# Thirty-two unused bytes in front of each weight slice of a fused attention and MLP kernel

## The chip, the cores and the metric

The kernel runs on one core of one Trainium2 chip. The metric is the device time of one execution in microseconds (us). A core has a matrix engine (PE, whose loads of the stationary operand are listed apart as PEld), three elementwise engines (DVE, ACT, POOL), a sequencer that issues most transfers (SP), and 16 DMA engines. Operands of the engines lie in the on-chip memory: 128 partitions, in each of which a buffer has the same byte address. Matmuls write to PSUM, a second small memory. This case is about the byte addresses of some of those buffers alone.

## The reference

Chunked attention on 4 batches, 8 heads, 768 positions and 64 values a head, and behind it an MLP on the 3072 tokens with 512 inputs, 2048 hidden units and 512 outputs, all in 32-bit floats:

```
for c in range(nc):                       # 24 chunks of 32 queries
    k_ctx = k[:, :, l_start:r_end]        # 16 keys to the left, 8 to the right
    k_full = np.concatenate([mem_k, k_ctx], axis=2)    # and 8 memory keys
    scores = scale * np.matmul(q_c, k_full.transpose(0, 1, 3, 2))
    a = np.exp(scores - np.max(scores, axis=-1, keepdims=True))
    a = a / (np.sum(a, axis=-1, keepdims=True) + 1e-09)
    out[:, :, c_start:c_end] = np.matmul(a, v_full)
...
h = x @ w_in
g = np.maximum(h, 0.0) + alpha * np.minimum(h, 0.0)
return g @ w_out
```

## The kernel before

The tokens go through the MLP in seven blocks: four of 384 tokens, then three of 512. The hidden dimension is cut into 16 slices of 128 units (f = 0 to 15). A step of the program is one block with one slice: an up product (x times the slice of w_in, line 746), the bend of the leaky ReLU (lines 755 and 758), and a down product (the result times the slice of w_out, line 776), which adds to the block's output over all 16 slices.

To keep 32-bit accuracy on a faster matmul format, each operand is split in a high and a low part (xh and xl, gh and gl, and w with its index 0 or 1), and each product is three matmuls: high by low, low by high, high by high. In the up product the weight is the stationary operand, loaded 128 columns (512 bytes a partition) at a time, and x is streamed past it, 384 or 512 columns. In the down product it is the other way round: 128 columns of g are stationary and the 512 columns of w (2048 bytes a partition) are streamed.

The weights stay on the chip. Slice f has a buffer in a pool of its own, `w{f}_0` (8192 bytes a partition; slices 0 and 1 have two pools of 4096 bytes each, `w0_0`, `w0_1` and so on). Such a buffer has up to three tenants one after the other. Those of slices 8 to 15 first hold the queries, keys and values of the first eight attention units (tile `early`: lines 502 to 508 load it, lines 324 and 579 multiply it). Then the raw 64-bit weights land in each (tile `w_t`, line 620), and a decode of five to six instructions on ACT, DVE and POOL turns them into a high and a low part in the same place (lines 643 to 672, tile `w`; the last instruction, line 672, writes the low part). From there on every step reads them.

The order of the work is set by a planner (class `Plan`): each step has an engine, an assumed cost, the buffers that it reads and writes, and a due time, and the planner hands out the steps by a simulated schedule before the program is emitted. Addresses are no input to it.

Pools are laid out in the order in which they are opened, one behind the other. Before the change the x buffers (pool `xp`), the bent hidden values and their parts (pools `gp`, `dec`, `tmp`, and the spare thirds of `xp`) and all weight slices start at addresses that leave 416 when divided by 512. The pieces that matmuls of lines 746 and 776 read within them begin at multiples of 512 bytes, so stationary and streamed operand of each of these matmuls begin at the same address modulo 512.

Of the kernel before, what the change touches and what calls it, by code (L numbers as in the profile page):

```python
# [9 lines left out]
F32 = mybir.dt.float32  # L10
# [8 lines left out]
P = 128  # L19
# [14 lines left out]
NF = DF // P  # L34
# [81 lines left out]

NAPART = 2


GATHER_ACT, HIGH_ACT = range(2, 14), 24  # L120

# [63 lines left out]
def body(ctx: ExitStack, tc: tile.TileContext, qvw, kw, whole, heads, w_in, w_out, alpha, out):  # L185
# [7 lines left out]
    sm = ctx.enter_context(tc.tile_pool(name="sm", bufs=1))  # L193
    xp = ctx.enter_context(tc.tile_pool(name="xp", bufs=1))
    gp = ctx.enter_context(tc.tile_pool(name="gp", bufs=1))
    wps = {(f, i): ctx.enter_context(tc.tile_pool(name=f"w{f}_{i}", bufs=1))
           for f in range(NF) for i in range(2 if f < NAPART else 1)}
    dec = ctx.enter_context(tc.tile_pool(name="dec", bufs=1))
    tmp = ctx.enter_context(tc.tile_pool(name="tmp", bufs=1))
    ps_h = ctx.enter_context(tc.tile_pool(name="ps_h", bufs=1, space=bass.MemoryType.PSUM))  # L200
# [785 lines left out]
```

## Time and profile before

| | |
|---|---|
| time, median of 2 runs | 595.97 us (595.90 to 596.05) |
| span of the profiled execution, first to last instruction | 593.9 us |
| TensorE clock granted over the span | 1.000 |
| PE busy | 586.2 us (99%) |
| PEld busy | 503.4 us (85%) |
| DVE busy | 390.2 us (66%) |
| ACT busy | 207.8 us (35%) |
| POOL busy | 47.5 us (8%) |
| moved by DMA | 47.65 MB |

The profile is of one execution; its span is 2.1 us under the median of the times, which also hold what lies before the first and behind the last instruction. Times within a view count from the start of the span. A row of a group gives the line, engine, operation, the output tile, an arrow, the input tiles, sizes and count, then busy time and the mean duration in ns. Matmuls overlap, so the duration of one (389 ns for 512 columns) is longer than the distance from one to the next; that distance is read from the chain of waits, which lists runs of matmuls with their start, length and count.

### The profile page before, as it was taken

The numbers are of one execution on the slowest core, as the hardware profiler recorded it, in microseconds if no ns is written. First come the engines' busy times: TensorE is split into PE (matmuls) and PEld (weight loads), VectorE is DVE, ScalarE is ACT, GpSimd is POOL, SyncE is SP. The second block draws the span as 40 slices with busy tenths as digits, with TensorE's granted clock in tenths as the row PEclk, the third lists the DMA queues.
The fourth block names the chain that finished last, engine by engine and source line by source line (L and its number), as shares of the span: only waits on it lengthen the run. The fifth ranks groups of instructions, "written<-read, shape, count | busy, mean of one in ns | idle before, by whom it ended". The sixth has DMA issues, their size and how long they took to land.

```text
span 593.9 us, 10980 instructions
## 1 busy us (share of the span) xinstructions
PE 586.2 (99%) x4407; PEld 503.4 (85%) x4407; DVE 390.2 (66%) x905; ACT 207.8 (35%) x578; POOL 47.5 (8%) x74
## 2 busy tenths in 40 slices
PE   7999999999999999999999999999999999999997
PEld 4889898989998989989888888888888888888886
DVE  8979999886768768686895842851961771530530
ACT  3888887725131404424224202302400401210201
POOL 5640000010000101010010100100100100000000
PEclk9999999999999999999999999999999999999999
DMA  8999300222041221403304003004101000000001
GB/s 321 393 408 408 124 0 2 66 65 89 2 153 30 72 66 37 153 1 102 102 0 153 2 1 100 2 0 133 40 1 36 0 1 36 36 1 0 2 0 71
DMA packets 21187, 47.65 MB, mean 80 GB/s; under 512 B 2576, under 2 KB 5904, under 8 KB 21136
## 3 DMA queue, kind: packets, MB, share of 16 engines
q1 hardware_dynamic: 20992, 46.83, 22.2%
q8 instruction: 34, 0.56, 0.4%
q14 instruction: 17, 0.14, 0.1%
q10 hardware_dynamic: 144, 0.13, 0.1%
HBM read 40.66 MB, written 6.29 MB: 79 GB/s over the span
## 4 chain that ended last, share of the span: by engine, by line
PE 97%; DMA 1%; POOL 1%; issue 0%; ACT 0%; SPq 0%; ACTq 0%; POOLq 0%
PE h_ps L746 45%; PE o_ps L776 44%; PE a_ps L450 3%; PE s_ps L349 2%; PE a_ps L579 1%; DMA early<-heads 1%; PE o_ps L566 1%; POOL early L211 1%; PE s_ps L324 0%; POOL ew L232 0%; ACT o_t L833 0%; ACT qk L571 0%; POOL eye L225 0%; POOL eye L224 0%; SPq L505 0%
## 5 line engine op out<-in xcount | busy, mean ns | idle before, releaser
L746 PE MATMUL h_ps<-xh,w 128*128 128x384 f32 (+1 forms) x896 | 248.8, 358 | 0.0
L746 PEld LDWEIGHTS h_ps<-xh,w 128*128 128x128 f32 x896 | 164.9, 188 | 16.0
L776 PE MATMUL o_ps<-w,gh 128*128 128x512 f32 x528 | 162.8, 389 | 0.0
L746 PE MATMUL h_ps<-xl,w 128*128 128x384 f32 (+1 forms) x448 | 162.7, 363 | 0.0
L755 ACT ACTIVATE g<-h_ps 128x384 f32<-128x384 f32 (+1 forms) x112 | 60.3, 538 | 193.1 <-PE h_ps L746 127.3
L758 DVE SCALAR_TENSOR_TENSOR g<-g,rise,h_ps 128x384 f32<-128x384 f32 (+1 forms) x112 | 74.9, 669 | 74.3 <-ACT g L755 73.3
L776 PEld LDWEIGHTS o_ps<-w,gh 128*128 128x128 f32 x528 | 99.1, 188 | 20.5
L425 DVE STREAM_TRANSPOSE pt<-e 32x192 f32<-32x192 f32 (+1 forms) x336 | 99.4, 301 | 7.4 <-POOL e L404 2.0
L776 PE MATMUL o_ps<-w,gl 128*128 128x512 f32 x264 | 102.8, 389 | 0.0
L746 PEld LDWEIGHTS h_ps<-xl,w 128*128 128x128 f32 x448 | 84.1, 188 | 10.1
L776 PE MATMUL o_ps<-w,xh 128*128 128x512 f32 x240 | 74.8, 393 | 0.0
L776 PEld LDWEIGHTS o_ps<-w,gl 128*128 128x128 f32 x264 | 49.6, 188 | 10.2
L489 DVE TENSOR_TENSOR xl<-a_ps,xh 128x384 fp32r<-128x384 f32 x32 | 17.5, 553 | 59.0 <-ACT xh L486 58.4
L404 POOL TENSOR_TENSOR e<-e,den 128x384 f32<-128x384 f32 x24 | 22.4, 931 | 408.6 <-DVE den L401 272.4
L776 PEld LDWEIGHTS o_ps<-w,xh 128*128 128x128 f32 x240 | 45.0, 188 | 8.9
L764 DVE CAST gh<-g 128x512 fp32r<-128x512 f32 (+1 forms) x72 | 29.0, 403 | 30.6 <-PE o_ps L776 28.1
L383 ACT ACTIVATE e<-s_ps,mx 128x64 f32<-128x64 f32 x144 | 43.4, 319 | 14.2 <-DVE mx L375 14.2
L486 ACT CAST xh<-a_ps 128x384 fp32r<-128x384 f32 x32 | 15.0, 482 | 95.2 <-PE a_ps L450 93.2
L768 DVE TENSOR_TENSOR gl<-g,gh 128x512 fp32r<-128x512 f32 (+1 forms) x72 | 46.9, 653 | 1.8
L776 PE MATMUL o_ps<-w,xl 128*128 128x512 f32 x120 | 46.7, 389 | 0.0
L383 ACT ACTIVATION_READ_ACCUMULATOR e<-s_ps,mx 128x1 f32 x144 | 30.6, 213 | 0.0
L833 ACT COPY o_t<-o_ps 128x512 f32<-128x512 f32 x21 | 12.1, 589 | 40.2 <-PE o_ps L776 39.8
(61 smaller groups left out, 381.3 us busy)
## 6 DMA issues: line engine op xcount, KB each, us to landing
w_t<-w_in SPq DMA_DIRECT2D x16, 512.0 KB, 10.1
w_t<-w_out SPq DMA_DIRECT2D x16, 512.0 KB, 10.2
qk<-kw SPq DMA_DIRECT2D x24, 272.0 KB, 4.3
v_t<-qvw SPq DMA_DIRECT2D x24, 256.0 KB, 2.8
out<-o_t SPq DMA_DIRECT2D x23, 256.0 KB, 2.0
qk<-qvw SPq DMA_DIRECT2D x24, 192.0 KB, 4.7
early<-heads SPq DMA_DIRECT2D x14, 232.0 KB, 4.9
early<-qvw SPq DMA_DIRECT2D x8, 256.0 KB, 5.8
```

Source lines behind the costliest of these rows:

```text
L383: nc.scalar.activation(out=st["e"][:, i], in_=st["s"][h2][:, n], func=AF.Exp, scale=SCALE, bias=d["mx"][:, u - us[0], n, h2:h2 + 1], accum ...
L404: nc.gpsimd.tensor_tensor(out=st["e"], in0=st["e"], in1=st["den"].broadcast_to([P, NJ * 2, KW]), op=ALU.mult)
L425: nc.vector.transpose(out=pts[u % NPT][quad * CH:(quad + 1) * CH, j, t0:t0 + n1 - n0].rearrange("p t h q -> p (t h) q"), in_=(st["e"], zer ...
L450: nc.tensor.matmul(out=st["a"][h2 * D:(h2 + 1) * D, t * TQ:(t + 1) * TQ], lhsT=st["v"][:, t, h2, :], rhs=pts[u % NPT][:, :, t, h2, :], sta ...
L486: nc.scalar.copy(out=ring[k][0][:, cols], in_=st["a"][:, :BT])
L489: nc.vector.tensor_tensor(out=ring[k][1][:, cols], in0=st["a"][:, :BT], in1=ring[k][0][:, cols].bitcast(F32), op=ALU.subtract)
L746: nc.tensor.matmul(out=h["ps"][:, :n_cols], lhsT=ws[f, 0][:, wk, k * P:(k + 1) * P], rhs=parts(blk, k)[1](xk), start=(k == 0 and n == 0), ...
L755: nc.scalar.activation(out=h["g"], in_=h["ps"][:, :n_cols], func=AF.Relu, scale=-1.0)
L758: nc.vector.scalar_tensor_tensor(out=h["g"], in0=h["g"], scalar=rise[:, f:f + 1], in1=h["ps"][:, :n_cols], op0=ALU.mult, op1=ALU.add)
L764: copy(out=h["gh"], in_=h["g"])
L768: nc.vector.tensor_tensor(out=h["gl"], in0=h["g"], in1=h["gh"].bitcast(F32), op=ALU.subtract)
L776: nc.tensor.matmul(out=o_ps[tt], lhsT=h[gk][:, tt * P:(tt + 1) * P], rhs=ws[f, 1][:, wk], start=(f == first_f and i == 0), stop=(f == last ...
```

## The change

In front of each slice's buffer a small pool is opened, with one tile of 32 bytes a partition in it. Nothing ever writes or reads this tile.

```diff
+STEP = 32
...
-    wps = {(f, i): ctx.enter_context(tc.tile_pool(name=f"w{f}_{i}", bufs=1))
-           for f in range(NF) for i in range(2 if f < NAPART else 1)}
+    wps = {}
+    for f in range(NF):
+        shift = ctx.enter_context(tc.tile_pool(name=f"shift{f}", bufs=1))
+        shift.tile([P, STEP // 4], F32, name=f"shift{f}")
+        for i in range(2 if f < NAPART else 1):
+            wps[f, i] = ctx.enter_context(tc.tile_pool(name=f"w{f}_{i}", bufs=1))
```

Slice f moves up by 32 × (f + 1) bytes: modulo 512 the slices now start at 448, 480, 0, 32, 64 and so on, up to 384 and 416 for slices 14 and 15. The pools behind them (`dec`, `tmp`) move by 16 × 32 = 512 bytes and keep their 416; the pools in front do not move. The instructions of every engine, their order, their waits and their shapes are the same as before; nothing differs but the addresses inside them.

## The prediction

> **What bounds the kernel now.** I read the page first, for which engine sets the end, then the chain of waits for what the engine spends its time on, then the engine's own waits.
>
> ```profile
> span 593.9 us, 10980 instructions
> ...
> PE 586.2 (99%) x4407; PEld 503.4 (85%) x4407; DVE 390.2 (66%) x905; ACT 207.8 (35%) x578; POOL 47.5 (8%) x74
> ...
> PE 97%; DMA 1%; POOL 1%; issue 0%; ACT 0%; SPq 0%; ACTq 0%; POOLq 0%
> PE h_ps L746 45%; PE o_ps L776 44%; PE a_ps L450 3%; PE s_ps L349 2%; PE a_ps L579 1%; DMA early<-heads 1%; PE o_ps L566 1%; POOL early L211 1%; PE s_ps L324 0%; POOL ew L232 0%; ACT o_t L833 0%; ACT qk L571 0%; POOL eye L225 0%; POOL eye L224 0%; SPq L505 0%
> ```
>
> PE is 97% of the chain that ends last, and 89% of the span is the two weight products, lines 746 and 776. The waits of PE over the whole span are these three:
>
> ```profile
> PE h_ps L308 <- DVE busy L214: 2.0, 1, 2.0
> PE s_ps L324 <- DMA early<-heads: 1.2, 3, 0.6
> PE s_ps L324 <- DVE den L544: 0.7, 1, 0.7
> ```
>
> All three are in the opening with the attention units (lines 308 and 324). Afterwards nothing that another engine does is waited for, so the time can change much in one way only: the distance from one matmul to the next changes. The groups of PE by shape give the number of matmuls of which a weight slice is one operand:
>
> ```profile
> L776 PE MATMUL o_ps<-w,gh 128*128 128x512 f32 x528 | 162.8, 389 | 0.0
> L746 PE MATMUL h_ps<-xh,w 128*128 128x384 f32 x512 | 130.5, 335 | 0.0
> L746 PE MATMUL h_ps<-xh,w 128*128 128x512 f32 x384 | 118.3, 389 | 0.0
> L776 PE MATMUL o_ps<-w,gl 128*128 128x512 f32 x264 | 102.8, 389 | 0.0
> L746 PE MATMUL h_ps<-xl,w 128*128 128x384 f32 x256 | 87.5, 342 | 0.0
> L746 PE MATMUL h_ps<-xl,w 128*128 128x512 f32 x192 | 75.2, 392 | 0.0
> L776 PE MATMUL o_ps<-w,xh 128*128 128x512 f32 x240 | 74.8, 393 | 0.0
> L776 PE MATMUL o_ps<-w,xl 128*128 128x512 f32 x120 | 46.7, 389 | 0.0
> ```
>
> The counts add up to 2496 (768 of 384 columns, 1728 of 512). The chain in order of time gives their distances; its columns are start, length, what, count:
>
> ```profile
> 78.62 2.10 PE h_ps L746 x12
> 80.72 2.08 PE o_ps L776 x9
> ...
> 149.76 6.26 PE h_ps L746 x36
> ...
> 546.77 21.76 PE h_ps L746 x96
> 568.53 21.77 PE o_ps L776 x96
> ```
>
> At the end of the span 96 matmuls of 512 columns take 21.76 us, 226.7 ns each, whether the weight is stationary (line 746) or streamed (line 776). Thirty-six of 384 columns take 6.26 us, 173.9 ns each. The difference is 52.8 ns for 128 columns, 0.412 ns a column; 512 columns at this rate are 211 ns, which leaves some 15 ns a matmul that don't depend on its length (rounding of the rows makes that 14 to 16). Earlier, at 80.72, nine matmuls of 512 columns take 2.08 us, 231.1 ns each: 4.4 ns more than at the end. Two rows of busy time by stretch show what differs between the two places:
>
> ```profile
> 40.00:70.00 30.00, 30.00 (x153) 27.33 (x152) 28.01 (x39) 25.60 (x32) 1.28 (x2) 1.00 0.82 325
> ...
> 500.00:594.00 94.00, 90.29 (x404) 74.39 (x400) 30.98 (x50) 14.72 (x26) 0.00 (x0) 1.00 0.06 23
> ```
>
> Columns are the stretch, its length, busy time of PE, PEld, DVE, ACT and POOL, the granted clock and the DMA share. In the early stretch DVE is busy 28.01 of 30.00 us and DMA 0.82 of the time; in the late one 30.98 of 94.00 and 0.06; the clock is 1.00 in both. So a matmul is slowed a little, by 4.4 ns in 227, by something that other users of the memory do. That is the only sign in this trace that the memory is felt by PE at all.
>
> **The change part by part.** It removes no instruction and adds none, no wait and no transfer. It moves sixteen buffers, and with them the addresses in four kinds of instructions. I take each kind for itself.
>
> *Matmuls and weight loads of lines 746 and 776.* Before, the stationary and the streamed operand begin at the same address modulo 512; now they differ by 32 to 480 bytes in 15 slices, and slice 15 (416 again) stays as it was. So 15/16 of 2496, 2340 matmuls, are touched. Can the start distance matter? A row of the weight loads:
>
> ```profile
> L776 PEld LDWEIGHTS o_ps<-w,gh 128*128 128x128 f32 x528 | 99.1, 188 | 20.5
> ```
>
> A load goes through 512 bytes a partition and takes 188 ns, under a matmul that goes through 2048 bytes in 227 ns. While one load lasts, the stream advances by some 2048 × 188/227 = 1700 bytes and the load by 512: their distance grows by about 1190 bytes, more than twice 512. Whatever distance the two begin with, every distance modulo 512 comes up twice during each load (once or less, if part of the 188 ns is only delay). If meeting at some distance cost anything, it would be met before and after the change alike. I therefore take nothing for this term. Its bounds from rows: the 15 ns that don't depend on the length are all that a better address could give back, 2340 × 15 ns = 35.1 us; as much again is my bound above. These ends are the rivals below and not part of the likely case.
>
> [...]
>
> *Crowding by other engines.* The 4.4 ns are paid where slices are decoded and loaded. The down matmuls whose other operand is in xh or xl are for the most part the early ones: 240 + 120 = 360, × 4.4 ns = 1.6 us. The up matmuls of that time go at 2.10/12 = 175.0 ns against 173.9, 1.1 ns more; for some 400 of them that is 0.4 us. Together 2.0 us: other addresses could take it away or double it. I take no change, since the decode writes and reads whole 8192-byte buffers and so passes over all addresses modulo 512 in any case. If the cover is gone (a neighbour that now always meets PE), it is the 2.0 us again.
>
> [...]
>
> *The decode (lines 643 to 672).* Its instructions read and write the moved buffers on ACT, DVE and POOL. It has next to no slack at slice 2, the first whose low part DVE makes:
>
> ```profile
> 39.57 1.23 DVE L672 TENSOR_TENSOR w<-a,w 128x1024 fp32r<-128x1024 f32 x1 [0.65 <-ACT w L667]
> ...
> 40.83 0.34 PE L746 MATMUL h_ps<-xl,w 128*128 128x384 f32 x1
> 40.85 0.35 PEld L746 LDWEIGHTS h_ps<-xh,w 128*128 128x128 f32 x2
> ```
>
> DVE ends at 39.57 + 1.23 = 40.80, the first up matmul with this slice starts at 40.83 and the load of its low part at 40.85. A decode that is slower by some time up to here would thus hold PE for that time, once. How much one such instruction varies with its surroundings:
>
> ```profile
> L672 DVE TENSOR_TENSOR w<-a,w x14: 1182/1220/1227, 39.6 to 119.4; 128x1024 fp32r<-128x1024 f32 x14
> ...
> 20.00:40.00 20.00, 20.00 (x186) 17.47 (x179) 17.31 (x35) 16.77 (x34) 12.46 (x20) 1.00 1.03 406
> ```
>
> From 1182 to 1227 ns is 4%. Four per cent of DVE's 17.31 us between 20 and 40 us is 0.7 us, either way. All new addresses are still multiples of 32 bytes, as the old ones were, and the shapes are the same; I take nothing.
>
> *The loads into the buffers.* `early<-heads` is 1% of the chain, and PE waits 1.2 us on it. The two rows that say what the loads of weights cost later:
>
> ```profile
> early<-heads SPq DMA_DIRECT2D x14, 232.0 KB, 4.9
> ...
> w_t<-w_in SPq DMA_DIRECT2D x16, 512.0 KB, 10.1
> ```
>
> After the opening PE waits for no transfer, so the weights' 10.1 us to landing are covered by the decode that runs ahead and the work on slices that are there. For the opening I bound the term by its wait: 1.2 us less if it went, 1.2 us more if it doubled. The two halves of one such load already land at two different addresses modulo 512 (2176 bytes apart), and no slice's buffer was on a multiple of 512 before. I take nothing.
>
> The sum: 0 from the matmuls, 0 ± 2.0 from crowding, 0 ± 0.7 from the decode, 0 ± 1.2 from the opening, so 0 ± 3.9 us on the span of 593.9. What lies around the span (595.97 − 593.9 = 2.1 us) is untouched. The forecast is 596.0 us, from 592.1 to 599.9.
>
> **The rivals.** First, the common address is what costs the 15 ns, and the change gives them back. For it: the 15 ns are there in each matmul, in both roles of the weight, and before the change no matmul of lines 746 and 776 has operands at different addresses modulo 512, so the trace can't exclude it. Against it: the distance sweeps over all values during each load, as worked out above, and the same 15 ns for 384 and 512 columns look like a cost of changing the stationary operand. Its time: 596.0 − 35.1 = 561 us in full; it counts as faster by 2% (11.9 us) from 11.9/2340 = 5.1 ns a matmul.
>
> Second, the other side: the common address is the good one. Load and stream start within a few ns of each other; now they begin at the same place and part, and with a start distance of a few hundred bytes the stream, which is the quicker, overtakes the load in the middle instead of at its end. Place: each of the 2340 matmuls. Price: at the least the 4.4 ns that crowding shows, 10.3 us, 606 us; at the most a second 15 ns, 631 us. It decides from 5.1 ns a matmul too. For it speaks only that 4.4 ns are seen to be lost to neighbours; against it, that the loads have 226.7 − 188 = 39 ns of room under a 512-column matmul, so a load that is a little slower would still be hidden.
>
> Third, the change doesn't do what it says, because the unused tiles get no room. The slices of the changed program do lie at sixteen offsets modulo 512, so this has no chance left; its time would be 596.0 as well.
>
> **How the numbers follow.** A difference of 2% is about what a measurement of this kernel can tell from no change, and I use it as the bound of the classes: 584.0 to 607.9 us. The forecast with its range of 592.1 to 599.9 gets 0.84; something between, 584 to 592 or 600 to 608 (an address effect of 2 to 5 ns a matmul), 0.05; the first rival at over 2%, 0.06; the second at over 2%, 0.05. So faster 0.06, same 0.89, slower 0.05. The range is that of the forecast, rounded to 592 to 600; what it leaves out is 0.16.
>
> **What would show it.** In the profile of the changed kernel the runs of 96 matmuls at the end of the chain should again take 21.7 to 21.8 us, on line 746 and on 776, and a run of nine early ones 2.08 us; PE's waits should be the same three. The first rival would show as 96 matmuls in under 21.3 us, the second as over 22.2 us, both first in slices other than 15. A slower decode would show as a wait of PE on DVE at line 746 near 40 us. Any distance other than 226.7 ns at the end of the span, where the other engines are mostly idle, would make the prediction wrong in its main step.

## The result

The changed kernel takes 604.17 us (604.13 to 604.22), the kernel before 595.97 us: a ratio of 1.0138, with an interval of 1.0109 to 1.0168. It is 8.2 us slower, within 2% but outside the forecast range of 592 to 600, and the interval of 0.3% to either side leaves no doubt that it is slower.

The page of the changed kernel answers to the first rows shown of before:

```profile
span 602.4 us, 10980 instructions
...
PE 594.0 (99%) x4407; PEld 503.4 (84%) x4407; DVE 390.5 (65%) x905; ACT 208.2 (35%) x578; POOL 47.6 (8%) x74
```

The span grew by 8.5 us and PE's busy time by 7.8, while the busy time of the other engines and of the weight loads stayed where it was. PE's waits on others, which are again all in the opening (lines have moved down by six):

```profile
PE h_ps L314 <- DVE busy L220: 2.0, 1, 2.0
PE s_ps L330 <- DMA early<-heads: 1.9, 3, 0.8
PE s_ps L330 <- DVE den L550: 0.5, 1, 0.5
PE s_ps L330 <- issue: 0.4, 1, 0.4
```

They add up to 4.8 us against 3.9, so 0.9 us at most. The rest is not a wait at all. The chain in order of time (start, length, what, count):

```profile
22.73 1.58 PE h_ps L752 x9
...
79.05 2.12 PE h_ps L752 x12
81.17 2.09 PE o_ps L782 x9
...
150.47 6.30 PE h_ps L752 x36
...
321.08 22.46 PE h_ps L752 x96
...
554.22 22.25 PE h_ps L752 x96
576.47 22.38 PE o_ps L782 x96
```

The two last runs of 96 matmuls took 21.76 and 21.77 us before and take 22.25 and 22.38 now: 231.8 and 233.1 ns a matmul instead of 226.7. The 36 matmuls of 384 columns went from 6.26 to 6.30 us, 173.9 to 175.0 ns, and the runs of nine early ones from 2.08 to 2.09.

Before, the first weight product and the first run of 96 matmuls began here:

```profile
22.43 1.56 PE h_ps L746 x9
...
318.55 22.01 PE h_ps L746 x96
```

That divides the growth of the span: the opening gave 22.73 − 22.43 = 0.3 us, the part up to the first run of 96 another (321.08 − 318.55) − 0.3 = 2.2 us, and the three wide blocks from there to the end (602.4 − 321.08) − (593.9 − 318.55) = 6.0 us. Those hold 1152 matmuls of 512 columns, 5.2 ns more for each. Of the 2.2 us in between, the distances from start to start give 2.0 us to the 512-column matmuls of the down products and 0.2 us to those of 384 columns.

Inside the last run of up products, each slice has twelve matmuls. Its timeline at the starts of slices 8, 9, 13, 14 and 15 and at the first down product:

```profile
554.05 0.39 PE L752 MATMUL h_ps<-xl,w 128*128 128x512 f32 x1
...
556.85 0.40 PE L752 MATMUL h_ps<-xl,w 128*128 128x512 f32 x1
...
568.03 0.40 PE L752 MATMUL h_ps<-xl,w 128*128 128x512 f32 x1
...
570.79 0.40 PE L752 MATMUL h_ps<-xl,w 128*128 128x512 f32 x1
...
573.59 0.39 PE L752 MATMUL h_ps<-xl,w 128*128 128x512 f32 x1
...
576.31 0.40 PE L782 MATMUL o_ps<-w,gl 128*128 128x512 f32 x1
```

Slice 8 takes 2.80 us (233 ns a matmul), slice 13 takes 2.76 (230), and slice 15, the one slice that kept its 416, takes 576.31 − 573.59 = 2.72 us, 226.7 ns, exactly as before the change. So the time hangs on the slice's address. Over all matmuls after 320 us, slices 256 bytes apart behave alike: from start to start, up products of slices moved by 64 and by 320 bytes take 233.3 and 233.0 ns on average, by 192 and by 448 both 229.9, by 256 again 226.7. So slice 7, which moved by 256 bytes, is a second one that loses nothing.

The theory taken to the chip (D): what counts is the distance, modulo 256 bytes, between the start of a matmul's streamed operand and the start of the weight load that runs under it. Its rivals: the old absolute offset of 416 is a good one (A), or the variety of sixteen offsets is what costs (V).

### The profile page after: what moved, and what is told of

It is laid out like the page before. It is cut to its first block, busy times and chain, and to the rows that moved or that the text cites. A ratio compares the mean times of both kernels' runs of the same rounds, so it can differ in the third digit from the quotient of the medians.

```text
span 602.4 us, 10980 instructions
## 1 busy us (share of the span) xinstructions
PE 594.0 (99%) x4407; PEld 503.4 (84%) x4407; DVE 390.5 (65%) x905; ACT 208.2 (35%) x578; POOL 47.6 (8%) x74
## 4 chain that ended last, share of the span: by engine, by line
PE 97%; DMA 1%; POOL 1%; issue 0%; ACT 0%; SPq 0%; ACTq 0%; POOLq 0%
PE h_ps L752 45%; PE o_ps L782 44%; PE a_ps L456 3%; PE s_ps L355 2%; PE a_ps L585 1%; DMA early<-heads 1%; PE o_ps L572 1%; PE s_ps L330 1%; POOL early L217 1%; POOL ew L238 0%; ACT o_t L839 0%; POOL eye L231 0%; POOL eye L230 0%; SPq L511 0%; POOL e L236 0%
## 5 line engine op out<-in xcount | busy, mean ns | idle before, releaser
L782 PE MATMUL o_ps<-w,gh 128*128 128x512 f32 x528 | 165.3, 394 | 0.0
L782 PE MATMUL o_ps<-w,gl 128*128 128x512 f32 x264 | 104.3, 395 | 0.0
```

The costliest lines, as they stand in the source:

```text
L782: nc.tensor.matmul(out=o_ps[tt], lhsT=h[gk][:, tt * P:(tt + 1) * P], rhs=ws[f, 1][:, wk], start=(f == first_f and i == 0), stop=(f == last ...
```

## The experiments

**All slices moved together by 256 bytes**

```diff
+    shift = ctx.enter_context(tc.tile_pool(name="shift", bufs=1))
+    shift.tile([P, 256 // 4], F32, name="shift")
     wps = {(f, i): ctx.enter_context(tc.tile_pool(name=f"w{f}_{i}", bufs=1))
```

> All weight slices moved together by 256 bytes, one pad in front of the first slice and none between. Theory D (what costs time is the distance, modulo 256 bytes, between the address where a matmul's streamed operand starts and the address where the next weight load starts; distance 0 is free, others cost 3 to 8 ns a 512-column matmul): 596.0 us, runs of 96 late matmuls 21.76 us on both lines, as before the change. Rival A (the old absolute offset 416 modulo 512 is the good one): 604 us or so, as after the change. Rival V (sixteen different offsets are what costs): 596.0 us.

Measured: 595.93 us, ratio 0.9998 (0.9989 to 1.0008). The last run of its chain:

```profile
568.94 21.77 PE o_ps L778 x96
```

No slice is at 416 modulo 512 any more, and nothing is lost: A falls, as far as 256 bytes go. (The pools behind the slices, `dec` and `tmp`, move along by 256 bytes here, while x and the pool `gp` stay.)

**All slices moved together by 32 bytes**

```diff
...
+    shift.tile([P, 32 // 4], F32, name="shift")
     wps = ...
...
+    back.tile([P, 480 // 4], F32, name="back")
```

> All weight slices moved together by 32 bytes, so they share one offset (448), with 480 bytes behind them so that what lies behind keeps 416. Theory D: every slice is now at distance 32 or 224 from its partner; slices at these distances in the changed kernel went at 233.2 to 233.5 ns, so runs of 96 late matmuls take 22.4 us on both lines and the time is 605 us (8.2 us times 6.7/5.7 on the 512-column matmuls). Rival V: 596.0 us. Rival A: also 604 to 605 us.

Measured: 605.16 us, ratio 1.0152 (1.0135 to 1.0169). All slices share one offset here, so V falls too: one step of 32 bytes costs more than the sixteen offsets. Two rows of 384 columns and of early down products, and the last two runs of its chain:

```profile
81.02 2.08 PE o_ps L780 x9
...
150.19 6.26 PE h_ps L750 x36
...
555.09 22.40 PE h_ps L750 x96
577.50 22.42 PE o_ps L780 x96
```

Every wide matmul of the late runs takes 233.3 to 233.5 ns, on both lines; the ones of 384 columns pay nothing (6.26 us, as before), nor do the early runs of nine.

**x, g, the slices and what lies behind moved together by 32 bytes**

```diff
+    shift = ctx.enter_context(tc.tile_pool(name="shift", bufs=1))
+    shift.tile([P, 32 // 4], F32, name="shift")
     xp = ctx.enter_context(tc.tile_pool(name="xp", bufs=1))
```

> 32 bytes in front of the x buffers, so that x, g, the weight slices and everything behind them move together by 32 bytes and all start at 448 modulo 512. Theory D: all distances are 0 again, 596.0 us, runs of 96 in 21.76 us. Rival A: 604 to 605 us, as all_32. Rival V: 596.0 us.

Measured: 595.86 us, ratio 0.9997 (0.9988 to 1.0007). The slices lie at the very addresses modulo 512 that cost 9.2 us in the run before (448), but now their partners moved along:

```profile
568.65 21.77 PE o_ps L778 x96
```

This is the run that decides: the relation between the two operands counts and not where the slices lie.

**x and the slices moved by 32 bytes, g left in place**

```diff
...
+    shift.tile([P, 32 // 4], F32, name="shift")
     xp = ...
...
+    backg.tile([P, 480 // 4], F32, name="backg")
     gp = ...
...
+    shiftw.tile([P, 32 // 4], F32, name="shiftw")
     wps = ...
...
+    back.tile([P, 480 // 4], F32, name="back")
```

> x and the weight slices moved by 32 bytes (448), g and its parts left at 416: up products are at distance 0, late down products (their g parts lie in pools g, dec and tmp) at distance 32; early down products, whose g parts lie in the x buffers, at 0. Theory D: late runs of 96 take 21.76 us on the up line and 22.40 us on the down line; with all_32's 4.9 us for these 782 down matmuls the time is 600.9 us. Rival A (absolute offset of the slices): 604 to 605 us, both lines slow.

Measured: 600.88 us, ratio 1.0078 (1.0061 to 1.0095); 600.9 was expected (the 782 matmuls named there should read 792, the 528 + 264 whose other operand is in gh or gl; that changes the sum by under 0.1 us). The last two runs:

```profile
551.56 21.77 PE h_ps L754 x96
573.33 22.41 PE o_ps L784 x96
```

The same slice at the same address is free as the stationary operand of the up product, whose x moved along, and costs 6.7 ns a matmul as the streamed operand of the down product, whose g did not. The early down products, whose g lies in the x buffers and moved along, lose nothing either: a run of 18 near 102 us takes 4.12 us as before, and 4.19 us where the slices moved alone.

**Matmuls alone, 64 distances**

```diff
+REPEAT = 24
+WIDTHS = (512, 384, 256)
+STEPS = range(64)
...
+    for width in WIDTHS:
+        for d in STEPS:
...
+            for i in range(REPEAT):
+                lo = i % 4 * P + d
+                nc.tensor.matmul(out=t[:, :width], lhsT=stay[:, lo:lo + P], rhs=move[:, :width], ...)
```

> Nothing of the reference is computed: after one load and two copies, 24 matmuls each for 64 distances (0 to 252 bytes in steps of 4) between streamed and stationary operand, at 512, 384 and 256 columns, with a new stationary operand for each matmul and all other engines idle. Theory D: at 512 columns 226.7 ns a matmul at distance 0, and 230 to 234 ns at the multiples of 32 (the sign is that of a moved stationary operand: 256 minus 4 per step); between the multiples of 32 it says nothing. At 384 columns the changed kernel paid 0 to 1 ns, so 173 to 175 ns throughout. If the distance only matters because other engines use the memory at the same time, all 64 distances take the same time here.

Each distance has a run of 24 matmuls in the chain. The names end in two letters for the distance (aa is 0, ab 4 bytes, ai 32, and so on in steps of 4). Some of the wide runs, at 32, 120 and 212 bytes, some of 384 columns, at 0, 32, 40 and 224, and two of 256 columns, at 0 and 64:

```profile
52.65 5.60 PE wideai L209 x24
...
175.56 5.45 PE widebe L209 x24
...
303.41 5.67 PE widecb L209 x24
...
364.50 4.19 PE midaa L209 x24
...
398.15 4.17 PE midai L209 x24
...
406.49 4.30 PE midak L209 x24
...
599.91 4.24 PE midce L209 x24
...
633.41 2.87 PE slimaa L209 x24
...
678.81 2.73 PE slimaq L209 x24
```

With every other engine idle, 512 columns at 32 bytes take 5.60/24 = 233.3 ns, as in the whole kernel. So no other engine has a part in it. The multiples of 32 take 229 to 234 ns, as expected but for 192 bytes, which is 1 ns under. Between them the picture is not smooth: at 120, 144, 156, 204, 228 and 252 bytes the pace is 227 ns, at 212 it is 236. Nothing at 512 columns is quicker than 226.7. (The run at distance 0 itself stood first, in the opening, where 24 matmuls took 8.59 us, 358 ns each, and is made good in the next experiment.) At 384 columns the pace lies between 173.3 and 176.7 ns (4.16 to 4.24 us for 24) at the multiples of 32, and is 173.7 (4.17/24) at 32 itself, which fits that the kernel with all slices moved by 32 bytes paid nothing there; but 40 bytes cost 179 ns, so narrow matmuls are not free of the effect, and the expectation of 173 to 175 throughout was missed. At 256 columns the 64 distances take 113 to 123 ns, and there equal starts are not the best: 119.6 ns (2.87/24) at distance 0, where the last matmuls of the run still take 120, against 113.7 (2.73/24) at 64 bytes. So what holds for 512 columns can't be carried over to 256.

**Which pair counts**

```diff
+CASES = [("warm", lambda i: (0, 0)), ("equal", lambda i: (0, 0)), ("apart", lambda i: (0, 8)),
+         ("nextequal", lambda i: (8 * (i % 2), 8 * ((i + 1) % 2))),
+         ("ownequal", lambda i: (8 * (i % 2), 8 * (i % 2)))]
...
+            a, b = place(i)
+            lo = i % 4 * P + b
+            nc.tensor.matmul(out=t, lhsT=stay[:, lo:lo + P], rhs=move[:, a:a + 512],
...
```

The two numbers of a case, a and b, are the starts of the streamed and the stationary operand in 4-byte words.

> Nothing of the reference is computed: 48 matmuls of 512 columns for each of 30 cases of start addresses, all other engines idle. Theory D says that the pair that counts is the streamed operand and the weight load that runs under it, which is that of the next matmul. So: equal 226.7 ns, apart (load 32 bytes further) 233 ns; nextequal (each stream differs by 32 bytes from its own stationary operand, but begins where the next load begins) 226.7 ns; ownequal (each stream begins where its own stationary operand did, the next load 32 bytes off) 231 to 235 ns. If the pair that counts is a matmul's own two operands, nextequal is 233 and ownequal 226.7. together (both moved by 32 to 224 bytes): 226.7 ns all. stay and stream (one moved by 32 to 288 bytes): a stream moved by k equals a stationary operand moved by 256 minus k; 256 is 226.7 again and 288 equals 32.

The chain, 48 matmuls a case (together, stay and stream end in a letter for 32 bytes times its place in the alphabet):

```profile
18.46 10.89 PE equal L211 x48
29.35 11.19 PE apart L211 x48
40.54 11.35 PE nextequal L211 x48
51.89 11.12 PE ownequal L211 x48
...
95.75 10.91 PE togetherd L211 x48
...
195.38 10.99 PE stayf L211 x48
...
217.57 10.89 PE stayh L211 x48
228.46 11.19 PE stayi L211 x48
...
250.86 11.00 PE streamb L211 x48
...
317.89 10.88 PE streamh L211 x48
```

equal takes 10.89/48 = 226.9 ns, apart 233.1. Moving both operands changes nothing but a few matmuls at the start (10.91 us), moving either by 256 bytes changes nothing (stayh 10.89 us, streamh 10.88), and 288 bytes is like 32 (stayi 11.19 as apart, streami 11.22 as streama with 11.20): the period of 256 bytes is confirmed in these cases. So is the sign: a stream moved by 64 bytes takes 11.00 us, a stationary operand moved by 192 takes 10.99. But nextequal, where every stream begins where the load under it begins, takes 236.5 ns and not 226.7, so theory D was too simple. The pair of a matmul's own operands doesn't explain it alone either, since ownequal takes 232 ns. In both cases successive streams begin at different places; whether that, or a need for both pairs to agree, takes the fast pace away, these two cases can't tell.

**Changes of one operand in turns and in blocks**

```diff
+         ("loadblocks", lambda i: (0, 8 * (i // 8 % 2))),
+         ("loadturns", lambda i: (0, 8 * (i % 2))),
+         ("streamblocks", lambda i: (8 * (i // 8 % 2), 0)),
+         ("streamturns", lambda i: (8 * (i % 2), 0)),
+         ("bothblocks", lambda i: (8 * (i // 8 % 2), 8 * (i // 8 % 2))),
+         ("streamfar", lambda i: (64 * (i % 2), 0)),
...
```

> Nothing of the reference is computed: 48 matmuls of 512 columns a case, all other engines idle; each operand's start changes alone, by 32 bytes, in turns or in blocks of eight. Theory D' (a matmul's stream must agree, modulo 256 bytes, with the load that runs under it, and successive streams must also begin at the same place, which is what nextequal lacked): loadblocks changes between 226.7 ns (eight with the next load equal) and 233 ns (eight with the next load 32 off), and the change comes one matmul before the stationary operand itself changes; streamblocks the same, with an odd distance at each change; loadturns half and half; bothblocks 226.7 ns but for one or two matmuls after each change; streamturns slow throughout (231 ns or more). streamfar, loadfar and bothfar (changes of 256 bytes) 226.7 ns throughout. If the pair that counts were a matmul's own two operands, loadblocks would change together with the stationary operand.

```profile
40.62 11.06 PE loadblocks L212 x48
51.69 11.27 PE loadturns L212 x48
...
74.11 11.05 PE streamturns L212 x48
85.16 11.07 PE bothblocks L212 x48
96.22 10.90 PE streamfar L212 x48
```

In loadblocks the distances from start to start of single matmuls (226, 227, 227, 226, 227, 227, 235 ns in one block) show that the slow pace begins with the last matmul before the stationary operand changes, so it is the load that runs under a stream, the next one, that disturbs. When the stationary operand changes back, two matmuls are still slow (233 and 231 ns) before the pace is 226 again. Changes of 256 bytes are harmless here too (streamfar 10.90 us, loadfar 10.88, bothfar 10.89, equal 10.89). But bothblocks, expected at 226.7 but for one or two matmuls after each change, takes 230.6 ns, streamturns 230.2 where 231 or more was expected, streamblocks 232, and loadturns 234.8 instead of half and half. In bothblocks every pair agrees again as soon as both starts have changed, and still the next matmuls are slow: five after a change back (230, 236, 229, 232, 231 ns, then 227), and all seven up to the next change after a change by 32 bytes (230, 224, 231, 236, 228, 233, 230). In the cases together of the run before, which stay at their new place, it is four or seven, then 227. So a change of start costs by itself, and the pace depends on the matmuls before and not on one pair of addresses alone. Only the rule that held in every run at 512 columns is taken from here: when all streams and all loads keep beginning at the same address modulo 256 bytes, the pace settles at 226.7 ns.

**The same in bf16**

```diff
-    move = const.tile([P, 896], F32R, name="move")
-    stay = const.tile([P, 896], F32R, name="stay")
+    move = const.tile([P, 896], BF16, name="move")
+    stay = const.tile([P, 896], BF16, name="stay")
...
-                lo = i % 4 * P + d
+                lo = i % 4 * P + 8 * d
```

> The same as the first bench with both operands in bf16 (a load goes through 256 bytes, a stream of 512 columns through 1024) and distances of 0 to 496 bytes in steps of 16. No theory says how large an effect is with half the bytes; if two reads that meet in the memory are the cause, some distances are slower than others here too, by less; if only the 4-byte format is affected, all 32 take the same time.

```profile
11.72 5.18 PE wideab L209 x24
...
293.20 3.90 PE midbf L209 x24
```

All distances take the same: 5.18/24 = 215.8 ns at 512 columns and 162.5 at 384 (the first run, in the opening, is slower as before, 6.66 us). Of these two formats only the 4-byte one shows the effect; whether by its bytes or by something else in it, this run doesn't tell.

## Why the prediction was wrong

*The step that failed* is the first term of the sum, "Matmuls and weight loads of lines 746 and 776", taken as nothing because the distance between load and stream "sweeps" over all values during each load. The term measures 2.2 + 6.0 = 8.2 of the 8.5 us by which the profiled span grew. The sweep argument treated the cost as a sum over meetings within one load. The runs show another kind of behaviour: the pace settles into a fixed pattern (226 and 227 ns throughout, or, in the up products of slice 12 of the changed kernel, moved by 416 bytes, 232, 237 and 231 ns in turns, to one ns) which depends on where stream and load begin, and on the starts of the matmuls before. How these patterns come about stays open, as does why 384 columns at 32 bytes pay nothing where 512 pay 6.6 ns.

One premise of the sweep is wrong as well, that a load reads evenly for its 188 ns. In the run of 256 columns at 64 bytes the loads are these:

```profile
L209 PEld LDWEIGHTS slimaq<-move,stay x24: 187/188/188, 678.5 to 681.2; 128*128 128x128 f32 x24
```

Twenty-four loads of 188 ns stand in 2.73 us, one every 114 ns, so neighbours overlap by 74 ns. If they read one after the other, a load reads for at most 114 ns, and the distance grows by at most some 520 bytes instead of 1190 (an estimate, by the prediction's own working with 114 for 188). That still passes every distance modulo 256, so this error alone doesn't explain the miss.

*The second rival had the place right*, that the common address is the good one, and its lower price of 4.4 ns and 606 us is near what came: 5.2 ns for the wide matmuls of the late blocks. That it came so near is luck, since the 4.4 ns were a misreading (below), and the 768 matmuls of 384 columns, which it charged as well, pay next to nothing (0.2 us together). I gave it 0.05 beyond 2% and 0.05 to all address effects of 2 to 5 ns, in both directions. Its reason, a quicker stream overtaking the load, isn't shown by any run, and that a distance of 256 bytes costs nothing speaks against it (595.93 us in all_256). Against it I had held the 39 ns of room under a load; the room doesn't help, since the loads don't become longer but the matmuls come later: PEld is busy 503.4 us in both profiles, 188 ns a load, and PE 7.8 us longer.

*The first rival* fell. The 15 ns that don't depend on the length are still there at the best address, and no distance of 64 in steps of 4 bytes gives any of them back at 512 columns. 10.9 of them go with the format, since bf16 with a new load for each matmul goes at 215.8 ns.

*The term "Crowding" was a misreading.* I took 231.1 ns in early runs of nine for a slowing by other engines. Longer runs of the same trace of before say otherwise:

```profile
101.65 4.12 PE o_ps L776 x18
...
156.02 10.24 PE o_ps L776 x45
...
205.13 12.28 PE o_ps L776 x54
```

Over 226.7 ns a matmul, 18, 45 and 54 matmuls take 0.04 us more, as nine do (2.08 − 9 × 0.2267 = 0.04). It is a fixed 40 ns a run, whatever its length, paid after the change from 384 to 512 columns: in the run of 45 the first nine distances from start to start are 229, 233, 236, 224, 231, 236, 228, 233 and 231 ns, and from there on 226 to 227. Runs of nine never reach the fast pace, and so had little to lose: 2.08 us became 2.09. So the sign was in the quoted rows, and I gave it to the wrong cause. These rows thus show nothing of other engines: the 40 ns are the same at 80 us and at 205 us, and with all other engines idle a distance of 32 bytes costs what it costs in the kernel. What the pace does follow is where the loads begin: in bench2, 226.9 ns against 233.1 for loads that start 32 bytes further.

*The other terms* held. The decode's busy time is unchanged (DVE 390.2 and 390.5 us, POOL 47.5 and 47.6), and no wait of PE on DVE appeared near 40 us. The opening came to 0.3 us, inside its ± 1.2; the runs that lost nothing show the same start of the first weight product (22.73 us where everything moved by 32 bytes), so it isn't worth a cause.

*The test named in advance* worked: "any distance other than 226.7 ns at the end of the span, where the other engines are mostly idle" is what the profile showed, with slice 15 as the control inside the same run, and the second rival's sign, over 22.2 us for 96 matmuls, came too (22.25 and 22.38). The bound of 2% for what a measurement can tell was too wide: 1.4% stands clear of an interval of 0.3%.

## What to carry to other kernels

For matmuls of 512 columns in this 4-byte format with a new stationary operand each time, let the starts of streamed and stationary operands agree modulo 256 bytes (226.9 ns a matmul here, 233.1 at 32 bytes); buffers of whole multiples of 256 bytes, one behind the other, do this without a thought, and a small odd buffer in between undoes it for everything behind (595.93 us with one of 256 bytes in front of the slices, 605.16 with one of 32). At 384 columns equal starts are among the best too (174.6 ns, of 173.3 to 179.2 over the 64 distances); at 256 columns they are not (119.6 against 113.7 ns), so try other distances there. Where a group of matmuls is a few ns over its best, compare the excess of short and long runs before blaming a neighbour: one that doesn't grow with the length, as the 40 ns of 9 to 54 matmuls here, is a start-up cost. And the argument that a cost averages out failed here by 8.2 us, because the pace settled into a pattern.

## What the runs showed of the hardware

- In the 4-byte format the start addresses of PE's stream and load set its pace: for 512 columns 226.7 to 226.9 ns at distances of 0 and 256 bytes (the kernel before, all_256, bench2), mostly 229 to 236 ns elsewhere (bench, over 24 matmuls), with six odd distances (120, 144, 156, 204, 228 and 252 bytes for a moved load) at 226.7 to 227.1. At 256 columns distance 0 is not the best: 119.6 ns against 113.7 at 64 bytes (bench).
- Moving both operands by 32 to 224 bytes costs nothing that lasts (10.91 us for 48 matmuls against 10.89, bench2), and bf16 shows no effect over distances in steps of 16 bytes: 215.8 ns for 512 columns at each of the 31 behind the opening, 162.5 for 384 at all 32 (bench_bf16).
- The pace has a memory: after both starts change together by 32 bytes and stay there it is regained after four or seven matmuls (bench2); after a change from 384 to 512 columns it takes nine, a loss of some 40 ns a run (the run of 45 at 156.02 us of the kernel before).
- Loads that the profile gives 188 ns each follow one another every 114 ns at 256 columns (bench), so they overlap.
